# Recurrence and mixture of experts: where the second expert's first rows are gathered

## The chip, the cores and the metric

One core of one Trainium2 chip. The metric is the device time of one execution in microseconds; runs are compared by their median.

## The reference

The inputs are six arrays for 4 batches, 8 heads, 768 steps and a head width of 40, and the weights of 8 experts. First a recurrence over the steps with a 40 x 40 state for each batch and head, then a top-1 mixture of experts on its output:

```python
for t in range(S):
    y[:, :, t] = einsum('bhd,bhde->bhe', rt, state)
    Sa = einsum('bhde,bhe->bhd', state, at)
    state = state * wt - outer(Sa, bt) + outer(vt, kt)
x = y.transpose(0, 2, 1, 3).reshape(3072, 320)      # tokens
e_idx = argmax(x @ w_gate); gate_w = softmax(x @ w_gate) at e_idx
out[tokens of e] = gate_w * sigmoid(x @ w_output_gate)[e] * (relu(x @ w1[e]) @ w2[e])   # 320 -> 1024 -> 320
```

All of it is float32.

## The kernel before

The recurrence is worked through in 12 chunks of 64 steps, each in two parts (batches of two) called q = 0 and 1. A chunk's preparation, the solve for its inner dependence and the output of the chunk before run interleaved (class Att). Each part's output tile `x` (128 tokens of 320) is written to a scratch array `xd` in DRAM, and at once its router logits are computed (Moe.route, lines 643 to 662).

After chunks 3, 7, 10 and 11 the tokens seen since the last time are assigned (Moe.pick, from line 664): VectorE finds each token's expert and its place in that expert's list, and GpSimd (POOL) scatters, with one indirect DMA per 128 tokens (L730), a record of each token into a table `tab` in DRAM with 480 slots for each expert. These are 8, 8, 6 and 2 scatters. All write the same table, and each waits until the one before has landed.

An expert's 480 slots are 4 tiles of 120 (TS). Because the first two tiles of experts 0 and 1 are filled by tokens of chunks 0 to 7 only, they can be worked on early: Moe.slots reads the table a first time after chunk 7 (L878, on POOL's queue) and converts it on VectorE (L880 and L882) into the index `ti`. Moe.tokens then gathers the rows of `xd` for some tiles into `xg` by indirect DMAs on POOL (L818, one for each tile of 120 rows), transposes them on TensorE (L826, three k blocks, one transpose for each tile and block), and splits them into a high part on ScalarE (`xh`, L828) and a low part on VectorE (`xl`, L829). Moe.expert multiplies by w1 in 8 feature blocks f of eight matmuls each (L850, in high and low parts), applies the relu into a high part on ScalarE (`hh`, L854) and a low part on VectorE (`hl`, L855), then for each tile multiplies by w2 in 24 matmuls (L865 to L867), scales the rows on VectorE (L869), and scatters them to the output on POOL (L870).

Moe.early runs along with the last chunks of the recurrence: it loads and splits expert 0's weights, gathers and transposes expert 0's first two tiles in a small pool `tp0`, in which the tag `xg` has one buffer, and works feature blocks 0 to 5 of expert 0. Moe.experts runs after the recurrence: it opens its own pools (among them `tp` with two buffers of each tag), finishes blocks 6 and 7 of expert 0 and its output, and goes on with expert 1's first two tiles, the second halves of experts 0 and 1, and experts 2 to 7 with four tiles each. While one unit computes, the transposes of the next unit and the weight splits (L778 to L784) of the next expert are taken in turn with it (unit). The second halves need the whole table: Moe.slots reads it a second time, on SP's queue, after the last scatter has landed.

Each engine works its own queue in order. The order in these queues is made by a planner that runs through the program with its own clock and takes what is ready, in program order where several are; `issue_after` adds a fixed order in a few places. A tile's buffer is given out again when the last reader of its old content is done.

Of the kernel before, what the change touches and what calls it, by code (L numbers as in the profile page):

```python
# [9 lines left out]
F32 = mybir.dt.float32  # L10
# [571 lines left out]
E, CAP, DM, FF, NTOK = 8, 480, 320, 1024, 3072  # L582
TS = CAP // 4
# [3 lines left out]
class Moe:  # L587
# [216 lines left out]
            for _ in range(lag):  # L804
                yield

    def tokens(s, tabs, e, t0, nt, pool, psx):

        nc = s.nc
        m = 2 if pool is s.tp0 else 4  # L810
        rows = 256 * (s.HALF + 1) if t0 + nt <= s.HT else NTOK
        xh = pool.tile([128, 3, TS * m], F32R, name="xh", tag="xh")[:, :, 0:TS * nt]
        xl = pool.tile([128, 3, TS * m], F32R, name="xl", tag="xl")[:, :, 0:TS * nt]
        xg = pool.tile([TS, m, DM], F32, name="xg", tag="xg")
        tb, ti = (x[:, :, 4 * e + t0:4 * e + t0 + nt] for x in tabs)
        yield tb, ti, xh, xl
        for t in range(nt):
            nc.gpsimd.indirect_dma_start(out=xg[:, t], out_offset=None, in_=s.xd[0:rows],  # L818
                                         in_offset=bass.IndirectOffsetOnAxis(ap=ti[:, 0, t:t + 1], axis=0),
                                         bounds_check=rows - 1, oob_is_err=True)  # L820
        yield
        for k in range(3):
            n = 128 if k < 2 else 64
            pt = psx(TS * nt)
            for t in range(nt):
                nc.tensor.transpose(out=pt[0:n, TS * t:TS * t + TS], in_=xg[:, t, 128 * k:128 * k + n],  # L826
                                    identity=s.ident[0:TS, 0:TS])
            nc.scalar.copy(out=xh[0:n, k], in_=pt[0:n])  # L828
            nc.vector.tensor_tensor(out=xl[0:n, k], in0=pt[0:n], in1=xh[0:n, k].bitcast(F32), op=ALU.subtract)  # L829
            if k == 2:  # L830
                nc.scalar.copy(out=xh[64:128, k], in_=pt[0:64])
                nc.scalar.copy(out=xl[64:128, k], in_=xl[0:64, k].bitcast(F32))
            yield

    def expert(s, nt, W, T, pool, ps1, ps2):

# [48 lines left out]
    def early(s, ctx, psx, mark):  # L885

        pool = lambda n, b: ctx.enter_context(s.tc.tile_pool(name=n, bufs=b, side="right"))
        s.wpa, s.tp0 = pool("wpa", 1), pool("tp0", 1)
        with s.tc.tile_pool(name="sp0", bufs=2, side="right") as sp:
            w = s.weights(0, s.wpa, sp, 12, mark)  # L890
            s.W0 = next(w)
            yield from w
        while not s.half:
            yield
        for _ in range(30):
            yield
        with s.tc.issue_after(mark['ds']):
            s.tabs = s.slots(s.tp0, s.nc.gpsimd)
        t = s.tokens(s.tabs, 0, 0, 2, s.tp0, psx)
        T = next(t)  # L900
        next(t)
        for _ in range(40):
            yield
        with s.tc.issue_after(mark['y']):
            next(t)
        yield from t
        s.hp0 = ExitStack()
        hp = s.hp0.enter_context(s.tc.tile_pool(name="hp0", bufs=E0, side="right"))
        s.hp = hp, TS * 2
        s.wait = {}  # L910
        s.E0 = s.expert(2, s.W0, T, lambda: s.hp, lambda: s.ps1(), lambda: s.ps2())
        s.ps1 = lambda: psx(CAP)
        for _ in range(4):
            next(s.E0)
            yield
        while 'over' not in mark:
            yield
        at = dict(a=mark['a'], b=s.at['g', 11, 0], c=mark['c'], d=s.at['t', 11, 1], e=s.at['g', 11, 1], f=s.at['p'])
        s.pins = {(4 + i // 8, i % 8): at[m] for i in range(8 * (E0 - 4)) for m in 'adee'[i // 4]}
        for _ in range(4, E0):  # L920
            next(s.E0)
            yield
        s.pins = {}

    def experts(s, ctx, verdict):
        tc = s.tc
        pool = lambda n, b, **k: ctx.enter_context(tc.tile_pool(name=n, bufs=b, **k))
        tp, wpb, sp, hp = pool("tp", 2), pool("wpb", 1), pool("sp", 4), pool("hp", 9)
        pp = pool("mps", 2, space=PSUM)
        psx = lambda n: pp.tile([128, CAP], F32, name="px", tag="px")[:, 0:n]  # L930
        ps1 = lambda: pp.tile([128, CAP], F32, name="ph", tag="ph", bufs=3)
        ps2 = lambda: pp.tile([TS, DM], F32, name="po", tag="po", bufs=3)
        s.hp, s.ps1, s.ps2 = (hp, CAP), ps1, ps2
        W, T = {0: s.W0}, {}

        def tok(tabs, *u):
            t = s.tokens(tabs, *u, tp, psx)
            T[u[:2]] = next(t)
            next(t)
            return t  # L940

        def wts(e, **k):
            w = s.weights(e, s.wpa if e % 2 == 0 else wpb, sp, **k)
            W[e] = next(w)
            return w

        def unit(e, t0, nt, prep):

            for _ in s.expert(nt, W[e], T[e, t0], lambda: s.hp, ps1, ps2) if (e, t0) != (0, 0) else s.E0:
                next(prep, None)  # L950
            for _ in prep:
                pass

        t = tok(s.tabs, 1, 0, 2)
        w = wts(1, st=s.st1)
        tabs = s.slots(tp)
        t2 = tok(tabs, 0, 2, 2)
        unit(0, 0, 2, chain(t, w))
        s.wait = None
        s.hp0.close()  # L960
        t3 = tok(tabs, 1, 2, 2)
        unit(1, 0, 2, t2)
        verdict(psx(1)[0:1])
        t = tok(tabs, 2, 0, 4)
        unit(0, 2, 2, t3)
        unit(1, 2, 2, chain(wts(2), t))
        for e in range(2, E):
            n = e + 1 < E
            t = tok(tabs, e + 1, 0, 4) if n else iter(())
            with ExitStack() as order:  # L970
                if not n:
                    order.enter_context(tc.manual_schedule(engines={mybir.EngineType.PE}))
                w = wts(e + 1) if n else t
                unit(e, 0, 4, chain(islice(w, 3), t, iter("  "), w) if n else t)
# [177 lines left out]
```

## Time and profile before

| | us |
|---|---|
| median of 3 runs (684.51 to 687.52) | 686.28 |
| the profiled execution's own time | 687.68 |
| its span, first to last instruction | 685.9 |
| TensorE busy | 633.7 |
| VectorE busy | 465.5 |
| ScalarE busy | 339.3 |
| GpSimd (POOL) busy | 228.0 |

Times in the rows are microseconds from the start of the span. TensorE's matmuls are pipelined, so one in the queue may start before the one before it has ended. The recurrence ends near 439 us; what follows are the experts. The clock granted to TensorE is 0.969 of the full one on average.

### The profile page before, as it was taken

The numbers are of one execution on the slowest core, as the hardware profiler recorded it, in microseconds if no ns is written. First come the engines' busy times: TensorE is split into PE (matmuls) and PEld (weight loads), VectorE is DVE, ScalarE is ACT, GpSimd is POOL, SyncE is SP. The second block draws the span as 40 slices with busy tenths as digits, with TensorE's granted clock in tenths as the row PEclk, the third lists the DMA queues.
The fourth block names the chain that finished last, engine by engine and source line by source line (L and its number), as shares of the span: only waits on it lengthen the run. The fifth ranks groups of instructions, "written<-read, shape, count | busy, mean of one in ns | idle before, by whom it ended". The sixth has DMA issues, their size and how long they took to land. (4 is left out here: it accounts for less than half of the span.)

```text
span 685.9 us, 21154 instructions
## 1 busy us (share of the span) xinstructions
PE 633.7 (92%) x8871; PEld 566.5 (83%) x8871; DVE 465.5 (68%) x911; ACT 339.3 (49%) x783; POOL 228.0 (33%) x337
## 2 busy tenths in 40 slices
PE   7686988898999999989999789889999999999996
PEld 6475877777988788888889779789999998999986
DVE  8868689959986997799399554463675445654231
ACT  2577752774378357637743354243563335343120
POOL 9655321341244356315214100425333133202112
PEclk9668999999999999999999999999999999999999
DMA  6995762276346626633225563163575444431001
GB/s 141 174 191 123 180 158 70 80 165 166 98 133 165 143 74 170 175 86 101 80 80 147 170 161 88 33 197 88 172 217 145 144 133 126 138 106 45 19 11 32
DMA packets 56305, 84.45 MB, mean 123 GB/s; under 512 B 26848, under 2 KB 43515, under 8 KB 54763
## 3 DMA queue, kind: packets, MB, share of 16 engines
q1 hardware_dynamic: 52331, 74.05, 41.3%
q0 software_dynamic: 3872, 8.97, 4.6%
q8 instruction: 72, 1.18, 0.7%
q14 instruction: 30, 0.25, 0.1%
HBM read 67.59 MB, written 8.96 MB: 112 GB/s over the span
## 5 line engine op out<-in xcount | busy, mean ns | idle before, releaser
L855 DVE SCALAR_TENSOR_TENSOR hl<-ph,hh 128x480 fp32r<-128x480 f32 (+1 forms) x74 | 41.2, 566 | 66.6 <-ACT hh L854 54.9
L854 ACT ACTIVATE hh<-ph 128x480 fp32r<-128x480 f32 (+1 forms) x74 | 36.5, 501 | 95.5 <-PE ph L850 83.6
L870 POOL DMA_INDIRECT out_dram<-y,ti x32 | 33.7, 1054 | 141.3 <-DVE y L869 87.0
L865 PE MATMUL po<-w2h,hh 128*120 128x320 f32 x256 | 78.7, 313 | 0.2 <-ACT hh L854 0.2
L866 PE MATMUL po<-w2l,hh 128*120 128x320 f32 x256 | 77.9, 310 | 0.0
L850 PE MATMUL ph<-xh,w1h 128*128 128x480 f32 (+1 forms) x222 | 76.6, 349 | 0.3 <-DVE base L700 0.3
L850 PE MATMUL ph<-xl,w1h 128*128 128x480 f32 (+1 forms) x222 | 76.1, 346 | 0.0
L867 PE MATMUL po<-w2h,hl 128*120 128x320 f32 x256 | 75.2, 309 | 0.0
L225 PE MATMUL pl<-Am,KBt 120*128 120x192 f32 (+1 forms) x288 | 62.7, 351 | 8.6 <-ACT LA L238 6.6
L240 POOL TENSOR_SCALAR_AFFINE_SELECT LA<-LA 64x192 f32<-64x192 f32 x144 | 54.1, 408 | 45.8 <-ACT LA L238 44.5
L383 ACT ACTIVATE As<-pa,hq 128x320 f32<-128x320 f32 x80 | 42.0, 528 | 48.0 <-PE pa L392 34.2
L236 ACT ACTIVATE N<-pl 32x192 f32<-32x192 f32 (+1 forms) x138 | 51.5, 373 | 27.9 <-PE pl L225 12.9
L730 POOL DMA_INDIRECT tab<-rec,si x24 | 29.6, 1235 | 91.7 <-DMA tab<-rec,si 40.0
L480 PE MATMUL pY<-KB,M 128*64 128x64 f32 (+1 forms) x768 | 54.4, 226 | 4.9 <-DVE M L468 3.5
L225 PEld LDWEIGHTS pl<-Am,KBt 120*128 120x128 f32 x288 | 47.0, 205 | 14.2 <-ACT LA L238 9.0
L392 PE MATMUL pa<-As,Tc 64*32 64x40 f32 x1792 | 51.0, 204 | 4.9 <-ACT As L383 4.8
L480 PEld LDWEIGHTS pY<-KB,M 128*64 128x64 f32 x768 | 47.6, 139 | 8.9 <-DVE M L468 4.0
L479 PE MATMUL pY<-Sd,R 128*64 128x64 f32 (+1 forms) x704 | 54.9, 228 | 0.0
L464 PE MATMUL pM<-R,VU 128*128 128x128 f32 x384 | 52.3, 287 | 0.9 <-ACT VU L456 0.8
L392 PEld LDWEIGHTS pa<-As,Tc 64*32 64x32 f32 x1792 | 40.2, 112 | 14.7 <-ACT As L383 5.2
L850 PE MATMUL ph<-xh,w1l 128*128 128x480 f32 (+1 forms) x148 | 51.0, 345 | 0.0
L464 PEld LDWEIGHTS pM<-R,VU 128*128 128x128 f32 x384 | 46.5, 195 | 2.7 <-ACT VU L456 1.2
(198 smaller groups left out, 1559.9 us busy)
## 6 DMA issues: line engine op xcount, KB each, us to landing
D<-in_din_dram SPq DMA_DIRECT2D x12, 1080.0 KB
st<-in_w_dram SPq DMA_DIRECT2D x16, 512.0 KB
st<-in_w_dram SPq DMA_DIRECT2D x16, 480.0 KB
XS<-in_vt_dram SPq DMA_DIRECT2D x24, 256.0 KB
XU<-in_vt_dram SPq DMA_DIRECT2D x24, 256.0 KB
VU<-in_vl_dram SPq DMA_DIRECT2D x24, 208.0 KB
w<-in_win_dram SPq DMA_DIRECT2D x12, 371.2 KB
st<-in_w_dram SPq DMA_DIRECT2D x16, 256.0 KB
```

The source lines that it names most:

```text
L225: nc.tensor.matmul(pl[:, i, 0:nj], KBt[:, 6 * side + g0 + i].rearrange("p n t -> p (n t)"), Am[:, g0 + i:g0 + i + 6 * nj - 5:6, 0:64], sta ...
L236: s.mark['n', c] = nc.scalar.activation(out=nn, in_=pn, func=AF.Copy, scale=-1.0).ins
L240: g.affine_select(out=la[:, :, i], in_=la[:, :, i], pattern=[[0, nj], [1, C]], base=0, channel_multiplier=-1, compare_op=ALU.is_gt, fill=0.0)
L383: s.mark['as'] = nc.scalar.activation(out=x, in_=pa, func=AF.Copy, scale=s.hq[:, h:h + 1]).ins
L392: nc.tensor.matmul(pa[o + w:o + w + 32, i], m(p)[o:o + 64], x[o:o + 64, i, :], start=start, stop=True, tile_position=(o, o + w), skip_grou ...
L464: nc.tensor.matmul(pM[:, i], VU[:, h0 + i].rearrange("p n t -> p (n t)"), R[:, :, h0 + i], start=True, stop=True)
L479: nc.tensor.matmul(o, R[:, side, i, :], Sf[:, 40 * i:40 * i + w], start=True, stop=False)
L480: s.mark['y'] = nc.tensor.matmul(o, Ms[i // 4][:, i % 4, side, :], Kf[:, k:k + w], start=not c, stop=True).ins
L850: nc.tensor.matmul(ph, l, r, start=(i == 0), stop=(i == 7))
L865: nc.tensor.matmul(po, hh[f][:, ts_], w2h[:, f], start=(f == 0), stop=False)
L866: nc.tensor.matmul(po, hh[f][:, ts_], w2l[:, f], start=False, stop=False)
L867: nc.tensor.matmul(po, hl[f][:, ts_], w2h[:, f], start=False, stop=(f == 7))
```

## The change

The gather is taken out of Moe.tokens into a function of its own, Moe.rows. Moe.early calls it for expert 1's first two tiles as soon as expert 0's transposes are in the program. The call allocates `xg` in `tp0`, whose one buffer is the one that expert 0's rows were in. Moe.experts hands the tile to Moe.tokens, which then gathers nothing for this unit. The tiles of all other units are gathered as before.

```diff
-    def tokens(s, tabs, e, t0, nt, pool, psx):
+    def tokens(s, tabs, e, t0, nt, pool, psx, gp=None):
         ...
-        xg = pool.tile([TS, m, DM], F32, name="xg", tag="xg")
         tb, ti = (x[:, :, 4 * e + t0:4 * e + t0 + nt] for x in tabs)
         yield tb, ti, xh, xl
-        for t in range(nt):
-            nc.gpsimd.indirect_dma_start(out=xg[:, t], out_offset=None, in_=s.xd[0:rows],
-                                         in_offset=bass.IndirectOffsetOnAxis(ap=ti[:, 0, t:t + 1], axis=0),
-                                         bounds_check=rows - 1, oob_is_err=True)
+        xg = gp or s.rows(tabs, e, t0, nt, pool)
         yield
...
+    def rows(s, tabs, e, t0, nt, pool):
+        nc = s.nc
+        m = 2 if pool is s.tp0 else 4
+        rows = 256 * (s.HALF + 1) if t0 + nt <= s.HT else NTOK
+        xg = pool.tile([TS, m, DM], F32, name="xg", tag="xg")
+        ti = tabs[1][:, :, 4 * e + t0:4 * e + t0 + nt]
+        for t in range(nt):
+            nc.gpsimd.indirect_dma_start(out=xg[:, t], out_offset=None, in_=s.xd[0:rows],
+                                         in_offset=bass.IndirectOffsetOnAxis(ap=ti[:, 0, t:t + 1], axis=0),
+                                         bounds_check=rows - 1, oob_is_err=True)
+        return xg
...
     def early(s, ctx, psx, mark):
         ...
         yield from t
+        s.xg1 = s.rows(s.tabs, 1, 0, 2, s.tp0)
         s.hp0 = ExitStack()
...
     def experts(s, ctx, verdict):
         ...
-        def tok(tabs, *u):
-            t = s.tokens(tabs, *u, tp, psx)
+        def tok(tabs, *u, **k):
+            t = s.tokens(tabs, *u, tp, psx, **k)
...
-        t = tok(s.tabs, 1, 0, 2)
+        t = tok(s.tabs, 1, 0, 2, gp=s.xg1)
```

## Rows read from the trace of the kernel before

**Rows 1.** TensorE's waits, 385 to 470 us, then 456 us to the end: total, times, longest

```profile
PE pa L392 <- ACT As L383: 4.1, 2, 2.7
PE px L826 <- DMA xg<-xd,ti: 2.7, 2, 1.5
...
PE po L865 <- ACT hh L854: 0.2, 1, 0.2
```

**Rows 2.** Timeline of TensorE, 445 to 455 us: start, us, instructions, idle time before

```profile
445.34 0.27 PE L850 MATMUL ph<-xl,w1h 128*128 128x240 f32 x1
446.81 0.29 PE L826 MATMUL px<-ident,xg 120*128 120x120 f32 x1 [1.20 <-DMA xg<-xd,ti]
448.62 0.32 PE L826 MATMUL px<-ident,xg 120*128 120x120 f32 x1 [1.51 <-DMA xg<-xd,ti]
448.70 0.40 PE L850 MATMUL ph<-xh,w1h 128*128 128x240 f32 x1
...
454.39 0.31 PE L867 MATMUL po<-w2h,hl 128*120 128x320 f32 x1
```

**Rows 3.** Windows: busy by engine, then TensorE's granted clock, DMA share, GB/s

```profile
442.00:445.00 3.00, 1.81 (x16) 1.48 (x16) 2.46 (x20) 0.78 (x4) 2.19 (x3) 1.00 0.01 1
448.00:453.00 5.00, 4.38 (x22) 4.39 (x23) 3.04 (x4) 3.97 (x6) 0.00 (x0) 0.66 0.92 320
453.00:456.00 3.00, 3.00 (x23) 2.97 (x22) 2.94 (x5) 2.41 (x5) 1.00 (x1) 1.00 0.11 39
```

**Rows 4.** Timeline of POOL, 380 to 463 us

```profile
390.61 0.62 POOL L878 DMA_DIRECT2D tr<-tab  x1 [7.25 <-issue]
...
427.39 1.03 POOL L730 DMA_INDIRECT tab<-rec,si  x1 [31.25 <-DVE rec L727]
...
442.20 0.97 POOL L730 DMA_INDIRECT tab<-rec,si  x1 [1.41 <-ACT LG L655]
...
444.91 1.11 POOL L818 DMA_INDIRECT xg<-xd,ti  x1 [0.31 <-issue]
446.33 1.03 POOL L730 DMA_INDIRECT tab<-rec,si  x1 [0.30 <-issue]
453.10 1.00 POOL L730 DMA_INDIRECT tab<-rec,si  x1 [5.75 <-DMA tab<-rec,si]
459.45 1.09 POOL L870 DMA_INDIRECT out_dram<-y,ti  x1 [5.35 <-DVE y L869]
...
462.28 1.10 POOL L818 DMA_INDIRECT xg<-xd,ti  x1 [0.31 <-issue]
```

**Rows 5.** Timeline of TensorE: other transposes of gathered rows, and what follows

```profile
419.12 0.37 PE L826 MATMUL px<-ident,xg 120*64 120x120 f32 x2
...
466.36 0.37 PE L826 MATMUL px<-ident,xg 120*128 120x120 f32 x2
466.49 0.38 PE L866 MATMUL po<-w2l,hh 128*120 128x320 f32 x1
```

**Rows 6.** Timeline of SP's queue: the second read of the table

```profile
455.25 0.34 SPq L878 DMA_DIRECT2D tr<-tab  x1
```

**Rows 7.** Timeline of VectorE, 392 to 460 us

```profile
392.70 0.28 DVE L880 COPY tb<-tr 120x128 f32<-120x128 f32 x1
...
445.55 0.16 DVE L713 SCALAR_TENSOR_TENSOR si<-mem 128x2 int32<-128x2 f32 x1
...
452.64 0.40 DVE L855 SCALAR_TENSOR_TENSOR hl<-ph,hh 128x240 fp32r<-128x240 f32 x1
...
458.88 0.55 DVE L869 TENSOR_SCALAR y<-po,tb 120x320 f32<-120x320 f32 x1 [0.32 <-PE po L867]
459.35 0.27 DVE L880 COPY tb<-tr 120x128 f32<-120x128 f32 x1
459.65 0.20 DVE L882 CAST ti<-tb 120x64 int32<-120x64 f32 x1
```

**Rows 8.** An idle stretch of TensorE in the recurrence, and the window behind it

```profile
390.05 0.76 PE L392 MATMUL pa<-As,Tc 64*32 64x40 f32 x32 [2.66 <-ACT As L383]
...
390.00:395.00 5.00, 4.95 (x105) 4.66 (x107) 3.79 (x7) 2.29 (x4) 1.80 (x3) 0.66 0.54 144
```

More of the change, by code (lines that the diff above doesn't have):

```diff
@@ L805, in weights @@
                 yield
-    def tokens(s, tabs, e, t0, nt, pool, psx):
+    def tokens(s, tabs, e, t0, nt, pool, psx, gp=None):
         nc = s.nc
         m = 2 if pool is s.tp0 else 4
-        rows = 256 * (s.HALF + 1) if t0 + nt <= s.HT else NTOK
         xh = pool.tile([128, 3, TS * m], F32R, name="xh", tag="xh")[:, :, 0:TS * nt]
         xl = pool.tile([128, 3, TS * m], F32R, name="xl", tag="xl")[:, :, 0:TS * nt]
-        xg = pool.tile([TS, m, DM], F32, name="xg", tag="xg")
         tb, ti = (x[:, :, 4 * e + t0:4 * e + t0 + nt] for x in tabs)
         yield tb, ti, xh, xl
-        for t in range(nt):
-            nc.gpsimd.indirect_dma_start(out=xg[:, t], out_offset=None, in_=s.xd[0:rows],
-                                         in_offset=bass.IndirectOffsetOnAxis(ap=ti[:, 0, t:t + 1], axis=0),
-                                         bounds_check=rows - 1, oob_is_err=True)
+        xg = gp or s.rows(tabs, e, t0, nt, pool)
         yield
```

## The prediction

> **What bounds the kernel now.** I read the page's first table first: TensorE is the fullest engine by far. An average says nothing about one place, so next came TensorE's waits. From 456 us to the end it waits 0.2 us in all [rows 1]: in that stretch its queue alone sets the end, and a microsecond won ahead of it is a microsecond off the kernel, as long as nothing else becomes late. In the stretch ahead (385 to 470 us) the second largest entry, 2.7 us, is two waits of the transposes of the second expert's first rows for the DMA that brings these rows [rows 1]. The timeline of TensorE shows the place: feature block 6 of the first expert issues its last matmul at 445.34, the two transposes stand at 446.81 and 448.62, and block 7, which needs nothing of them, stands behind them in the queue until 448.70 [rows 2]. The windows show what follows: the granted clock is 0.66 on average from 448 to 453 us, so for part of it at the lower of the two levels (1.2 GHz), and full again from 453 [rows 3]. POOL's timeline shows why the rows are late: the second gather is issued at 444.91, right behind a chain of scatters into the slot table that ends with the one at 442.20, while the same queue has nothing to do for 31.25 us before 427.39 [rows 4].
>
> **The change part by part.**
>
> *The two gathers move.* They keep their size and count (2 DMAs of 120 rows). They no longer fill a tile of the later pool, but the first expert's tile, so each now waits until the first expert's six transposes have read it. Those end at 419.12 + 0.37 = 419.5 [rows 5]. POOL is idle then, so two gathers of 1.11 us with 0.31 between [rows 4] would run from about 419.5 to 422.1 and land by 424.7 (the second one's landing now takes 2.6 us: issued until 446.02, used at 448.62 [rows 2, 4]). Queued behind this wait on POOL are the six scatters of chunks 8 to 10, the first of which can't start before 427.39 because it waits for its records [rows 4]: 5.3 us of cover. If that cover were gone the price would be 2.8 us on the scatters, of which about 1.3 is slack: the last of the six starts at 442.20, and one takes 2.15 us from start to landing (453.10 to the read of the table at 455.25 [rows 4, 6]), so it is down at 444.35, and the next scatter needs slots that exist only at 445.55 + 0.16 = 445.71 [rows 7]. I take 0. The gathers' traffic moves to a stretch with fewer loads; I take 0 there too.
>
> *The wait goes.* With the rows there, the two transposes follow block 6 at once, 0.11 us after its last matmul's start. A pair takes 0.13 us at the full clock (466.36 to 466.49 [rows 5]), so block 7 starts at 445.45 + 0.13 = 445.58 and not at 448.70: **3.12 us**, the two waits and the pipeline's emptying around them. The step of 0.11 is an estimate from the pair; with a whole matmul of 0.27 [rows 2] it would be 2.96.
>
> *The low clock goes.* TensorE is busy without a break after 448.70, and from 448 to 453 the clock lacks 0.34 x 5 = **1.70 us** [rows 3]. That it does not fall in the changed kernel is a choice: it is 1.00 from 442 to 445 [rows 3], where TensorE is busy for only 1.81 of 3 us, and what it did before it fell is 2.7 us of waiting within 3.1. If it fell all the same, 1.70 would be lost again.
>
> So TensorE could be 3.12 + 1.70 = 4.82 us earlier at 453 us. Two things can be late in its place.
>
> *VectorE and ScalarE behind the transposes.* Their work for the second expert starts with the split of the transposed rows and so comes forward with the transposes, by 448.62 - 445.5 = 3.1, not by 4.82. The low part of block 7 is written at 452.64 + 0.40 = 453.04 [rows 7] and needed by the last matmul of the first output group at 454.39 [rows 2]; shifted, it is there at 449.94 and wanted at 449.57: **0.4 us** late. Bounds: 0 (the planner may order VectorE otherwise) to 1.72 (nothing had slack); I take 0.4, since it is worked out from the two rows.
>
> *The rows of the first expert's second half.* This is the next gather, and it hangs on the slot table: scatters at 446.33 and 453.10, read of the table at 455.25, its conversion on VectorE at 459.35 and 459.65, the second gather at 462.28 [rows 4, 6, 7]. That gather ends at 463.38, lands 2.6 later at 465.98, and the transposes stand at 466.36 [rows 5]: 0.38 us of slack today. How far does the chain come forward? (a) The conversion stands behind two output scalings on VectorE (the last is at 458.88 [rows 7]), which wait for TensorE. The table read itself should be down 2.1 us after its issue, as the other one was (390.61 to 392.70 [rows 4, 7]), so at 457.35: 2.0 us are won once the scalings are earlier. (b) The gathers then don't stand behind an output scatter, which ends at 459.45 + 1.09 = 460.54 [rows 4], 0.7 after the index at 459.85 [rows 7]: 0.7. (c) The scatter at 446.33 landed only just before 453.10, while the weight loads kept the DMA engines 0.92 full from 448 to 453 [rows 3]. Without two gathers of 154 KB each in that stretch, 307 KB at its 320 GB/s, it lands some 1.0 us earlier. Bounds of (c): 0.45 (only its issue comes earlier, to just behind the slots) and 4.5 (it lands 2.15 us behind an unhindered issue). The sum is 3.7.
>
> The rule for (c) that stands against me is in the Trainium skill, DMA: Bandwidth & Descriptors, section on queues, rings and completion order: a DMA engine takes turns between its queues packet by packet, so a small scatter would share turns with the loads and need not wait for a backlog to drain. By that, taking bytes out of the backlog brings the scatter little, and the sum would end at 3.5. The row (landing at the very moment at which the DMA share falls, 0.92 before 453 and 0.11 after) speaks more for the backlog.
>
> **The sum.** TensorE alone would be 4.82 - 0.4 = 4.4 us earlier; the chain of the next rows allows 3.7 + 0.38 = 4.1. The smaller gain counts: **4.1 us**. The profiled execution took 687.68 us, of which 685.9 are the span; 687.68 - 4.1 = 683.6. It stands 1.4 above the median of the three runs (686.28), so on the median the forecast is **682.2 us**, 0.6% less.
>
> **The rivals.**
>
> *The next gather takes the wait over.* If neither (a) nor (b) nor (c) holds, the chain of the slot table stays where it is, and TensorE gains only the 0.38 of slack; with (a) and half of (c) it gains 2.9. For it: the slack of 0.38 is small and the three terms are inferred. Against it: the conversion on VectorE starts right behind the scaling, which waited for TensorE. Middle of it: 1.6 us, 684.7.
>
> *The change does not do what it says.* The order of POOL's queue is planned, and if the gathers are put behind the scatters of chunks 8 to 10, they run where they run today: 0, 686.3. For it: the scatters belong to older work. Against it: their records come 8 us after the transposes.
>
> *Slower: one long hole in place of two short ones.* If the chain of the table does not come forward at all and gathers put between the scatters make it late (2.8 - 1.3 = 1.5), TensorE is 4.4 early at the transposes of the second half and waits 4.4 - 0.38 + 1.5 = 5.5 us in one piece. A single idle stretch of 2.66 us ahead of 390.05 was followed by a clock of 0.66 over 390 to 395, which is 0.34 x 5 = 1.7 us lost [rows 8]. Net: 1.5 - 0.38 + 1.7 = 2.8 us slower, 689.1. It decides from the point where the hole is as long as those 2.66 us. It needs the planner to interleave the queue badly, which the 31 us gap on POOL makes unlikely.
>
> **How the numbers follow.** Chances: forecast 0.52, the next gather takes over 0.28, no effect 0.08, slower 0.12. The forecast's own range is 3.0 to 5.2 us of gain (4.8 with nothing late, and 0.4 if transposes fill holes between 442 and 445 us; 3.0 with (c) at 0.45 and the clock partly low), 681.1 to 683.3. The range for 8 in 10 reaches over the takeover and no effect: 680.8 to 686.9. About 0.5% is what a measurement of this kernel can tell from no change, 3.4 us, or 682.85: most of the forecast's range lies below it and a part above, which, with half a chance in the forecast and the medians' own spread, gives faster 0.50. Same gets 0.40 (the takeover, no effect, the weak end of the forecast and the mild part of the slower case), slower 0.10.
>
> **What would show it.** In the changed trace the two gathers stand on POOL at 419 to 423 us, ahead of the scatter that waits for its records; the transposes' wait for their rows is gone from TensorE's waits; the granted clock is 1.00 from 445 to 455; the conversion of the table moves by about 3 us on VectorE. Wrong: a new wait of TensorE for gathered rows between 455 and 470 us of over 1.5 us (the takeover), a clock of 0.5 behind it (the slower case), gathers behind 427 us (no effect), or a tail after 470 us that is no longer free of waits.

## The result, and the profile after

In 14 runs of each, the changed kernel took 680.87 us in the median (678.15 to 689.2) and the kernel before 687.34 (683.41 to 693.79). The ratio is 0.9902, 95% interval 0.9878 to 0.9925: 1.0% faster, 5.2 to 8.4 us. A gain of 4.1 us was forecast. The sign and the mechanism were right, the size was too small. Here and below, a few executions in a slower state are left out of the ratios. The profiled execution took 678.98 us.

Every engine's queue has the instructions of before in the order of before; only POOL's differs, by the two gathers, which now stand ahead of the six scatters. Their place on POOL, with the chain behind them (columns as in [rows 4]; L838 is the gather, L878 the output scatter):

```profile
416.28 1.09 POOL L838 DMA_INDIRECT xg<-xd,ti  x1 [21.70 <-PE px L821]
417.67 1.09 POOL L838 DMA_INDIRECT xg<-xd,ti  x1 [0.30 <-issue]
423.89 1.03 POOL L730 DMA_INDIRECT tab<-rec,si  x1 [5.12 <-DVE rec L727]
...
442.14 0.97 POOL L730 DMA_INDIRECT tab<-rec,si  x1 [2.43 <-DVE si L713]
446.81 1.47 POOL L730 DMA_INDIRECT tab<-rec,si  x1 [3.70 <-DMA tab<-rec,si]
452.39 1.04 POOL L878 DMA_INDIRECT out_dram<-y,ti  x1 [4.11 <-DVE ti L890]
...
455.18 1.11 POOL L838 DMA_INDIRECT xg<-xd,ti  x1 [0.31 <-issue]
```

They wait for the first expert's transposes, and their issue is over 5.1 us before the scatters can start. TensorE around block 6 (against [rows 2] and [rows 5]):

```profile
440.66 0.35 PE L858 MATMUL ph<-xh,w1h 128*128 128x240 f32 x1 [0.34 <-DVE mem L704]
...
441.64 0.37 PE L821 MATMUL px<-ident,xg 120*128 120x120 f32 x2
441.77 0.36 PE L858 MATMUL ph<-xh,w1h 128*128 128x240 f32 x1
...
446.54 0.31 PE L875 MATMUL po<-w2h,hl 128*120 128x320 f32 x1
...
450.18 0.27 PE L858 MATMUL ph<-xh,w1h 128*128 128x240 f32 x1
...
457.86 0.37 PE L821 MATMUL px<-ident,xg 120*128 120x120 f32 x2
```

Block 7 follows block 6 after 1.11 us, pair of transposes included. From block 6 to the second expert's first matmul (450.18) there are 9.52 us; in the kernel before it was 444.49 to 458.69, 14.20:

```profile
444.49 0.35 PE L850 MATMUL ph<-xh,w1h 128*128 128x240 f32 x1 [0.34 <-DVE base L700]
...
458.69 0.27 PE L850 MATMUL ph<-xh,w1h 128*128 128x240 f32 x1
```

The windows (columns as in [rows 3]) show the clock at 1.00 throughout:

```profile
442.00:445.00 3.00, 3.00 (x25) 3.00 (x24) 2.23 (x4) 3.00 (x6) 0.97 (x1) 1.00 0.57 179
445.00:448.00 3.00, 3.00 (x23) 2.97 (x22) 2.94 (x4) 3.00 (x5) 1.19 (x1) 1.00 0.97 329
448.00:453.00 5.00, 5.00 (x41) 4.84 (x39) 4.33 (x9) 1.32 (x5) 0.89 (x2) 1.00 0.51 147
```

VectorE converts the table at 451.88, with no idle time ahead of it ([rows 7] had 459.35):

```profile
445.76 0.40 DVE L863 SCALAR_TENSOR_TENSOR hl<-ph,hh 128x240 fp32r<-128x240 f32 x1
...
451.88 0.26 DVE L888 COPY tb<-tr 120x128 f32<-120x128 f32 x1
```

From the second expert's first matmul to the last one (679.02 before, 670.27 now) the two profiles take nearly the same, 220.33 us before and 220.09 after. So the two profiles differ by 4.68 us in the stretch of the change and by 0.24 behind it. The rest of the 8.7 us between their spans arose ahead of 440 us, most of it (3.5) before the gathers' new place, where both run the same instructions: chance. But the timed runs say more than 4.7, so the question was where the other 1 to 2 us are.

### The profile page after: what moved, and what is told of

It reads as the page before. It is cut to its first block, busy times and chain, and to the rows that moved or that the text cites. A ratio compares the mean times of both kernels' runs of the same rounds, so it can differ in the third digit from the quotient of the medians.

```text
span 677.2 us, 21154 instructions
## 1 busy us (share of the span) xinstructions
PE 630.9 (93%) x8871; PEld 564.3 (83%) x8871; DVE 464.9 (69%) x911; ACT 340.2 (50%) x783; POOL 233.8 (35%) x337
## 5 line engine op out<-in xcount | busy, mean ns | idle before, releaser
L878 POOL DMA_INDIRECT out_dram<-y,ti x32 | 34.3, 1073 | 141.5 <-DVE y L877 80.8
L838 POOL DMA_INDIRECT xg<-xd,ti x32 | 35.8, 1118 | 44.6 <-PE px L821 32.7
```

## The experiments

All stretches below run from block 6's first matmul to the second expert's first. "Gather issued" is the start of the second gather's issue; this time and that of its transpose are counted from block 6. They are read from each kernel's timelines:

| profile | gather issued | its transpose | stretch |
|---|---|---|---|
| kernel before, on record | 0.42 | 4.13 | 14.20 |
| b3_before_p3 | 0.69 | 5.28 | 15.21 |
| b4_before_p4 | 0.81 | 5.67 | 16.71 |
| b2_before_p2 | 0.82 | 5.71 | 16.61 |
| b5_before_p5 | 0.99 | 5.79 | 17.08 |
| b2_before_p1 | -1.69 | 1.40 | 9.89 |
| changed, 4 profiles | -22.99 | 1.1 (pair) | 9.52 each |

What stands ahead of block 6 counts, too. From the first expert's first transposes to block 6 the changed kernel takes 27.07 us in all four profiles, and the kernel before 27.07 to 27.47 in the five with a hole: the gathers cost nothing in their new place.

**The kernel before, five more profiles.**

> The kernel before once more, for a second profile of its stretch from block 6 of the first expert to the second expert's first matmul, which took 14.20 us in the profile on record and 9.52 in three profiles of kernels with early gathers. Theory A (the landing of the second gather, and so the hole, differs from one execution to the next, and the profile on record had a short one): 15 to 17 us here. Theory B (the stretch always costs 4.7 us and the rest of the measured gain is elsewhere): 14.0 to 14.4 us.

> The kernel before, for a third profile, with the same expectations: theory A 15 to 17 us for the stretch, theory B 14.0 to 14.4 us.

> The kernel before, for a fourth profile. The stretch from block 6 to the second expert's first matmul took 14.20, 9.89 and 16.61 us in the three so far. Theory A (a race: the hole is there when the two gathers are issued later than the weight loads' start less some 2.5 us, and absent when the scatter chain ran 2 us ahead): the stretch is near 10 with gathers issued over 3 us before block 6, or 14 to 17 with gathers issued less than 1.1 us before it. Theory B (the hole has nothing to do with the time of issue): any other pairing.

> The kernel before beside them, a fifth profile. Theory A (race with the loads): the time from the second gather's issue to its transpose lies on the line of the other three, 3.7 at 0.42 us after the start of block 6 to 4.9 at 0.82, or no wait at all with an issue over 1.5 us before block 6. Theory B (no tie to the time of issue): off this line by over 0.6 us.

> The kernel before beside it, a sixth profile. Theory A: with the second gather issued 0.4 to 0.9 us after block 6 begins, 3.7 to 5.0 us from there to its transpose and a stretch of 14 to 17 us; with an issue over 1.5 us before block 6, no hole and a stretch near 9.9. Theory B: any other pairing.

The profile on record was the mildest of the five with a hole, as theory A had it, and one has next to none (9.89 us in b2_before_p1), which neither theory of that run foresaw; theory A of the later three takes it in, and they agree with it (b5_before_p5 at its edge). The longest hole, b5_before_p5: TensorE's wait, then the windows.

```profile
PE px L826 <- DMA xg<-xd,ti: 4.2, 2, 2.6
```

```profile
443.00:446.00 3.00, 1.22 (x9) 1.08 (x9) 1.74 (x15) 0.58 (x2) 2.39 (x3) 0.80 0.27 63
446.00:449.00 3.00, 0.44 (x2) 0.16 (x3) 0.00 (x0) 0.00 (x0) 0.55 (x1) 0.50 0.99 331
449.00:454.00 5.00, 5.00 (x22) 5.00 (x23) 3.57 (x5) 4.53 (x8) 1.46 (x1) 0.50 0.54 204
454.00:457.00 3.00, 3.00 (x20) 2.97 (x18) 2.97 (x4) 1.95 (x4) 0.04 (x1) 0.82 0.08 21
```

Its wait is 4.2 and not 2.7 us, and the clock is at the lower level for all of the 5 us behind it. The weight loads on SP are issued at 1.40 to 1.45 after block 6 in these five, because they wait for the slots that VectorE writes then. An issue takes 1.1 us, so the gather is still being issued when the loads start; the one on record has 0.1 us left, those issued 0.3 to 0.6 us later have more, and their rows take 4.6 to 4.9 us from issue to transpose and not 3.7. In b3_before_p3 and b5_before_p5 the trace has the landings: the first gather, whose issue ends 0.8 to 1.0 us ahead of the loads, lands 3.1 us after the start of its issue, the second one 4.5 and 4.8 us. POOL in b2_before_p1, the one without a hole:

```profile
437.88 0.97 POOL L730 DMA_INDIRECT tab<-rec,si  x1 [1.41 <-DMA tab<-rec,si]
439.16 1.13 POOL L818 DMA_INDIRECT xg<-xd,ti  x1 [0.30 <-issue]
440.60 1.11 POOL L818 DMA_INDIRECT xg<-xd,ti  x1 [0.31 <-issue]
443.78 1.03 POOL L730 DMA_INDIRECT tab<-rec,si  x1 [2.07 <-DVE si L713]
```

From the second on, its scatters follow each other every 2.4 us; in the others one of these steps takes 2.9 to 3.6. And TensorE is later: the recurrence's last but one output takes 0.8 us longer on its way from M to x (2.45 us, 1.7 in the others). So here the gathers come 2.1 us or more earlier against block 6, and are through before the loads begin. Such an execution is still behind the changed kernel: from the first expert's first transposes to the second expert's first matmul it takes 38.31 us (28.42 of them ahead of block 6), the changed kernel 36.59.

**The changed kernel again, three times.**

> The changed kernel itself, for more executions beside the others and a second profile of the stretch. Between the two profiles on record, the stretch from block 6 of the first expert to the second expert's first matmul is 4.7 us shorter, as the forecast's two terms on TensorE said (4.82), but the 14 runs say 6.7 us (5.2 to 8.4). Theory A (the hole in front of the transposes is longer in most executions than in the one profiled): 5.5 to 7 us faster again, with no wait for gathered rows and a clock of 1.00 here. Theory B (the measured effect was lucky, the true one is the 4.7 of the profiles): 4.2 to 5.2 us faster.

> The changed kernel beside them, as the yardstick on the same chip, and a third profile: 9.5 us from block 6 to the second expert's first matmul as in the other two (theory A), 4 to 7 us below the kernel before in most chips and less where the kernel before has executions without the hole.

> The changed kernel once more, on whatever chip comes, beside the kernel before. In the two calls where the kernel before ran at 687.7 and 686.7 us the changed one gained 0.9% and 0.8%; in the two where it ran at 683.9 us, three of its profiles or those of kernels with its order had the gathers issued 2.1 us earlier and no hole, and the changed kernel was not among the runs. Theory A (the gain is the hole, and there is less of it where the kernel before often escapes it): near 681 to 682 us in any case, 0.8 to 1.0% faster if the kernel before is near 687, and 0.2 to 0.6% if it is near 684. Theory B (the chip's level moves both kernels alike): 0.8 to 1.0% faster wherever the kernel before lies.

Medians 681.51, 682.09 and 679.71, ratios 0.9912 (0.9884 to 0.9941), 0.9917 (0.9886 to 0.9948) and 0.9897 (0.9855 to 0.9938). The stretch is 9.52 us in every profile. Against the five profiles with a hole that is 4.7 to 7.6 us, 6.4 in the mean; by their ratios the timed runs gave 5.7 to 7.1. The first of these runs alone (4.1 to 8.0 us) allows both of its theories; the four measurements together, weighted by their intervals, say 6.4 us (5.4 to 7.4), which is theory A: the missing 1 to 2 us are longer holes. On the two chips where the kernel before was profiled beside it, profile and time agree (5.69 and 5.7 us in b3, 7.56 and 7.1 in b5). Whether the gain shrinks on chips where the kernel before often has no hole could not be seen, and so the theories of b5_after can't be told apart: on these three chips it ran at 686.7 to 687.7 us. All four profiles with the gathers early in the old place (b2_before_p1, b2_held6 and both of b4_late_loads) are from two other chips, where it ran at 683.9 us and the changed kernel was not run.

**Only the place undone.** The kernel is the changed one, but with the gathers behind a given scatter:

```diff
-        s.xg1 = s.rows(s.tabs, 1, 0, 2, s.tp0)      # in early
...
+        with s.tc.issue_after(s.at['s', 8, 5]):     # in experts; the sixth scatter (3: the fourth, 4: the fifth)
+            s.xg1 = s.rows(s.tabs, 1, 0, 2, s.tp0)
```

> The changed kernel (rows in the first expert's tile) with the two gathers held on POOL behind the sixth scatter of chunks 8 to 10, their place in the kernel before; every queue has the order of the kernel before. Theory A (only the time of issue matters): as slow as before, within 0.4%, with the transposes waiting 2.5 to 5 us for their rows and the clock at half rate behind it. Theory B (the tile matters, since the later pool's tile also waits for memory of the recurrence): 2 to 5 us faster than before.

Ratio 1.0002 (0.9963 to 1.0041): the time of the kernel before, so the tile alone is worth at most 2.5 us here and probably nothing. The profile itself fell on an execution without a hole (issue at -1.69, stretch 10.04, 0.3 us of waiting), as did b2_before_p1 on the same chip, where the kernel before ran at 683.89 us. Theory A is right on the time; the hole it expected was not in this one profile. How much the place is worth on this chip is not shown, since the changed kernel was not run there.

> The same with the gathers held behind the fourth scatter only, so that the fifth and sixth scatter stand behind them. Theory A: the rows land at about the end of block 6, so TensorE's wait and the low clock are gone or nearly gone; the scatters end later, but the last of the six has slack and the two gathers then no longer stand ahead of the scatters of chunk 11: 4 to 6.5 us faster than before, within 1.5 us of the changed kernel. Theory B (gathers between the scatters make the slot table late, as the slower rival of the forecast has it): a new wait of TensorE of over 2 us between 455 and 470 us, and 0 to 3 us faster than before only.

Ratio 1.0038 (0.9998 to 1.0079), against both theories. The rows were there in time and the stretch was 9.52, but the recurrence's last output took 3.69 us from M to x in place of 1.35, with gaps that wait for nothing the profile shows:

```profile
PE pY L480 <- issue: 0.7, 2, 0.4
PE pY L479 <- issue: 0.6, 2, 0.3
```

From the first expert's first transposes to block 6 this profile takes 30.44 us, 3.4 more than the changed kernel, so what the stretch gained was lost ahead of it. The gathers' rows were moving just then, which was the reason for the next two runs.

> The changed kernel with the two gathers held on POOL behind the fifth of the six scatters of chunks 8 to 10. Behind the sixth, in the old place, the time was that of the kernel before; behind the fourth the rows were there in time (no wait, clock 1.00), but TensorE lost 2.3 us to gaps marked as issue in the last output of the recurrence while the gathers' rows were moving. Behind the fifth the gathers run some 2.5 us later, mostly after that output. Theory A (two things cost: rows that are not there at the end of block 6, and rows that move while the recurrence's last output is issued): no hole before block 7 and under 1 us of issue gaps, within 1 us of the changed kernel. Theory B (any place among the scatters costs): 2 us or more slower than the changed kernel.

> The changed kernel with two more gathers of the same rows, into a tile that nothing reads, behind the fourth scatter. Theory A (moving 307 KB by POOL's queue while TensorE issues the many small matmuls of the last output keeps TensorE's instructions from coming): the last output, from the second masked product M to x on VectorE, takes 3 us and more in place of 1.35, and the kernel is 1.5 to 3 us slower than the changed one. Theory B (the gaps in that stretch were chance): under 0.7 us slower, with the stretch at 1.3 to 1.8 us.

b3_extra4 adds two gathers that nobody reads behind the fourth scatter:

```diff
+        with s.tc.issue_after(s.at['s', 8, 3]):
+            s.rows(s.tabs, 1, 0, 2, s.tp0, "xq")
         t = tok(s.tabs, 1, 0, 2, gp=s.xg1)
```

Its last output took 1.35 us from M to x, so theory A of b3_extra4 is not borne out. But this does not clear the gathers: on the chips of b2 and b4 the last output takes 1.6 to 1.7 us in every other profile, whatever the kernel, on the chip of b3 1.35 in all four, so the chip may have a part in it. What stopped TensorE in b2_held4 stays open. Both kernels are slower than the changed one beside them in the median, by 1.4 us (b3_held5, between its two theories) and 1.0 us (b3_extra4), though the intervals overlap (0.9951, 0.9922 to 0.9981, and 0.9938, 0.9907 to 0.9970, against 0.9917, 0.9886 to 0.9948). In the profiles the reason is another one. VectorE and POOL in b3_held5:

```profile
447.44 0.99 DVE L877 TENSOR_SCALAR y<-po,tb 120x320 f32<-120x320 f32 x2
451.98 0.27 DVE L888 COPY tb<-tr 120x128 f32<-120x128 f32 x1 [3.54 <-DMA tr<-tab]
452.28 0.19 DVE L890 CAST ti<-tb 120x64 int32<-120x64 f32 x1
452.39 1.03 DVE L863 SCALAR_TENSOR_TENSOR hl<-ph,hh 128x240 fp32r<-128x240 f32 x3
```

```profile
436.49 1.03 POOL L730 DMA_INDIRECT tab<-rec,si  x1 [0.30 <-issue]
440.91 1.15 POOL L730 DMA_INDIRECT tab<-rec,si  x1 [3.39 <-DMA tab<-rec,si]
447.53 0.98 POOL L730 DMA_INDIRECT tab<-rec,si  x1 [5.47 <-DMA tab<-rec,si]
```

The sixth scatter stands behind the gathers, so the scatters of chunk 11 run at 440.91 and 447.53 (4.1 and 10.8 us after block 6, against 1.5 and 6.2 in the changed kernel), and the table is late. Its conversion is in VectorE's queue ahead of the second expert's `hl`, waits 3.54 us, and TensorE waits for `hl` (in b3_extra4 the same two waits are 3.52 and 2.19 us). That wait, and the clock behind it (columns as before):

```profile
PE ph L858 <- DVE hl L863: 2.2, 1, 2.2
```

```profile
445.00:450.00 5.00, 4.76 (x38) 4.57 (x38) 3.44 (x7) 1.27 (x6) 2.02 (x2) 1.00 0.09 32
450.00:455.00 5.00, 2.83 (x16) 2.55 (x16) 1.64 (x6) 0.65 (x3) 1.25 (x2) 0.85 0.82 218
455.00:460.00 5.00, 5.00 (x36) 5.00 (x35) 1.10 (x4) 1.25 (x4) 4.09 (x4) 0.81 0.48 140
```

This is the forecast's slower rival, in a milder form and through VectorE: from the second expert's first matmul to the last these two profiles take 224.03 and 225.28 us, against 220.32 in b3_after_ref. The medians differ by less, so these two executions were worse than most.

**Early gathers, with the old ones left in place.**

```diff
+        s.rows(s.tabs, 1, 0, 2, tp)
         t = tok(s.tabs, 1, 0, 2, gp=s.xg1)
```

> The changed kernel with the two gathers issued a second time at their old place, into a tile that nothing reads. The early rows are the ones used, so TensorE's wait is gone, but POOL's queue and the DMA traffic beside the weight loads are as before. Theory A (all of the gain is TensorE's wait and its clock): as fast as the changed kernel, within 0.5 us. Theory B (part of the gain is that the slot table's scatters and the next gather come earlier without the two gathers): 1 to 2.5 us slower than the changed kernel, with TensorE waiting for gathered rows between 455 and 470 us.

681.98 us, ratio 0.9924 (0.9896 to 0.9953), half a microsecond above the changed kernel beside it. The stretch is again 9.52, so the wait is what counts. But the table's conversion comes 1.4 us later against block 6 (12.73, 11.35 in b1_after_again), and the next gather's transposes wait longer than there. First this run, then b1_after_again:

```profile
PE px L821 <- DMA xg<-xd,ti: 0.9, 1, 0.9
```

```profile
PE px L821 <- DMA xg<-xd,ti: 0.5, 1, 0.5
```

So theory A for the time, and 0.4 us of theory B in the profile (0.8 in all from the second expert's first matmul to the last, 221.53 and 220.73): this is about what the traffic and POOL's queue are worth, by one execution of each.

**Late gathers, but other work ahead of the transposes that wait.**

```diff
-            for _ in s.expert(...) if (e, t0) != (0, 0) else s.E0:
-                next(prep, None)
+            for i, _ in enumerate(s.expert(...) if (e, t0) != (0, 0) else s.E0):
+                if (e, t0) != (0, 0) or i >= 2:
+                    next(prep, None)
```

> The kernel before with the gathers where they were, but with block 7 and the first output tile of the first expert ahead of the second expert's transposes in TensorE's queue, some 4.4 us of work. Theory A (the cost is only that work which needs none of the rows stands behind the wait): the wait of 2.7 us and the low clock go without an earlier gather, 4 to 6.5 us faster than before. Theory B (the lateness of the rows itself is on the path, since VectorE and ScalarE split them and the weights behind them): under 2 us faster, with new waits of TensorE for xh or xl near 455 us.

684.12 us, ratio 0.9954 (0.9924 to 0.9984): 3.2 us faster than before, half of the change's gain. The stretch is 9.95, but a new wait stands behind it, and on VectorE its cause:

```profile
PE ph L850 <- DVE xl L829: 2.3, 1, 2.3
```

```profile
453.41 0.27 DVE L880 COPY tb<-tr 120x128 f32<-120x128 f32 x1 [2.58 <-DMA tr<-tab]
453.60 0.71 DVE L829 TENSOR_TENSOR xl<-px,xh 128x240 fp32r<-128x240 f32 x2
```

Again the conversion of the late table blocks VectorE's queue, here for the second expert's `xl`. Each theory has half: TensorE's order removes the hole, and the late rows come back as a wait for `xl`.

**A hole with TensorE kept busy.**

```diff
+            if f == 6 and s.wait is not None:
+                fl = ps2()
+                with s.tc.issue_after(mm):                       # block 6's last matmul
+                    for _ in range(20):
+                        nc.tensor.matmul(fl, hh[0][:, 0:TS], w2h[:, 0], start=True, stop=True)
```

> The kernel before with 20 matmuls that nobody reads (some 2.9 us of work) between block 6 and the transposes that wait. The wait keeps its place and length, but TensorE is busy through it. Theory A (the clock falls because of the hole): the clock is 1.00 from 445 to 455 us and the time is 1.0 to 2.0 us below before. Theory B (the clock's fall is chance and not tied to the hole, or costs nothing): within 0.5 us of before.

687.75 us, ratio 0.9998 (0.9970 to 1.0025). In the profile the gather was issued at 0.77, its transpose still waited 1.4 us behind the filler, and the clock stayed at 1.00. The stretch is 14.08, where kernels before with an issue at 0.69 and 0.81 had 15.21 and 16.71. But a new wait of 0.8 us for the next gather's rows stands behind it, since the order of VectorE's queue changed too. So the stretch speaks for theory A and the time for theory B, whose interval reaches to 2.1 us faster. What the clock alone is worth is inconclusive.

**Weight loads held until the rows have landed.**

```diff
+        pr = s.dr.tile([TS, 8], F32, name="pr")
+        s.probe = nc.sync.dma_start(out=pr, in_=s.xg1[:, 1, 0:8]).ins    # xg1: the second expert's xg
...
+                    if st:
+                        order.enter_context(s.tc.issue_after(s.probe))
```

> The kernel before with one small store of the second gather's rows put ahead of the four weight loads in SP's queue, so that these loads (480, 320 and twice 512 KB) start only when the rows have landed; nothing else moves. In the kernel before the second gather took 3.7, 4.6 and 4.9 us from its issue to the transposes that wait for it when it was issued 0.42, 0.69 and 0.82 us after block 6 began, and the loads were issued 1.40 after it each time; the first gather took 3.2 to 3.3. Theory A (its rows stand behind the weight loads on the DMA engines, and the later it is issued the more of them): 3.2 to 3.5 us from issue to transposes whatever the time of issue, a stretch of 13.5 to 14.3 us, and 0.5 to 2 us faster than before. Theory B (the rows' landing does not depend on the loads): 3.7 to 4.9 us as before, a stretch of 14.2 to 16.6, no faster than before or slower by the later loads.

> The same kernel, a second profile, same expectations: theory A 3.2 to 3.5 us from the issue of the second gather to its transpose, theory B 3.7 to 4.9 us.

682.91 us, ratio 0.9984 (0.9960 to 1.0008), and 683.64 in the single execution of the second. In both profiles the gathers were issued early (-1.69), so there was no race to take away: inconclusive. The loads' part in the hole rests on the table and the landings above, not on an intervention, and it need not be the whole: in b1_second_gather the first of the late gathers landed only 4.6 us after the start of its issue, though that issue ended 1.0 us ahead of the loads. One profile showed something else: a wait of only 0.20 us, and yet a low clock behind it.

```profile
440.00:444.00 4.00, 2.59 (x22) 2.05 (x20) 2.37 (x14) 1.53 (x5) 2.86 (x3) 1.00 0.26 80
444.00:446.00 2.00, 1.75 (x12) 1.57 (x13) 1.55 (x14) 0.58 (x2) 0.46 (x1) 0.84 0.34 85
446.00:449.00 3.00, 3.00 (x15) 3.00 (x15) 2.12 (x4) 2.96 (x5) 0.96 (x2) 0.54 0.45 76
```

## Why the prediction was right in kind and wrong in size

- **The bound**: right. TensorE's queue alone sets the end from 456 us; whatever the stretch gained or lost arrived at the end (220.0 to 220.3 us from the second expert's first matmul to the last in every profile with no wait for rows, `xl` or `hl` in it, 220.7 to 225.3 in those with one).
- **The gathers' move**: right, at no cost (27.07 us ahead of block 6, not more than before), and at the place that was forecast (between the transposes and the scatter that waits for its records).
- **The wait**: the step that failed is that a single profile's hole was taken as the size. 3.12 us was right for that execution (block 7 at 4.21 us after block 6, now 1.11), but it was the shortest of five: block 7 stood at 5.41 in b3_before_p3 and at 5.92 in b5_before_p5, so this term is 3.1 to 4.8 us. One execution of six had next to none (0.15 us of waiting).
- **The low clock**: 1.70 was 1.58 in that execution (4.68 - 3.10), 1.39 in b3_before_p3 (5.69 - 4.30) and 2.75 with the longest hole (7.56 - 4.81). That it would stay at 1.00 was right in all four profiles of the changed kernel. The ground given, that short holes don't lower it, was weak: in b4_late_loads it fell after pauses without a long hole.
- **VectorE's 0.4 us**: not there. A row was misread: the matmul at 454.39 [rows 2] is that of block 6; the ones that need block 7's `hl` follow the transposes after it. In the changed kernel `hl` is written by 446.16 and wanted at 446.54.
- **The next rows' 0.3 us**: not there in this profile, so TensorE's 4.8 came through undiminished (4.68), but with nothing to spare. The chain came forward by 3.3 us at its second gather (17.79 us after block 6 before, 14.52 now), nearly the 3.7 that were forecast, though with other parts: (b) did not happen, the gathers still stand behind the output scatter at 452.39, and (c) was larger (the last scatter came 2.5 us earlier against block 6, not 1.0). What was wrong is the slack of 0.38: the two transposes at 466.36 [rows 5] need only the first of the two gathers. Those that need the second are the next pair, at 467.16. In the changed kernel these pairs stand at 457.86 and 458.66, and the second gather, issued at 455.18, lands 3.4 us later (the last number of its row), at 458.6, 2.3 us after the end of its issue:

```profile
467.16 0.37 PE L826 MATMUL px<-ident,xg 120*128 120x120 f32 x2
```

```profile
458.66 0.42 PE L821 MATMUL px<-ident,xg 120*128 120x120 f32 x2
```

```profile
xg<-xd,ti POOLq DMA_INDIRECT x1, 3.4
```

By the same 2.3 the slack before was about 1.5 us (463.38 + 2.3 against 467.16; an estimate, the profile before lacks this landing), and all of it is used up now. So it was in part luck that nothing was lost: in b1_after_again TensorE waits 0.5 us here, the rival of the takeover in a mild form.
- **The rule for (c) in the Trainium skill** (DMA: Bandwidth & Descriptors, section on queues, rings and completion order), that a small transfer shares turns with the loads and gains little from a smaller backlog. The trace of the changed kernel agrees with the first half: the scatter issued at 442.14 landed 3.9 us later, at 446.0, while the DMA engines stayed 0.97 full from 445 to 448. The row that was read against it was misread: the scatter of 446.33 [rows 4] stood behind two gathers in POOL's own queue. With them put back (b1_second_gather) it landed 5.8 us after its issue, and 3.9 in b1_after_again beside it; these 1.9 us are most of (c).
- **The slower rival** needs gathers between the scatters; put there, they made the table late as described, and cost 1.4 and 1.0 us in the medians against the changed kernel (b3_held5, b3_extra4; not clear of noise). Both are still faster than the kernel before.

In sum: the forecast's 4.1 and the 0.7 us of the two deductions that were not there make 4.8, of which the two profiles show 4.7; the 1 to 2 us that the timed runs show above that are holes longer than the one profiled.

What stays open: why in some executions the scatters run 2.1 us or more ahead (one step takes 2.4 and not 2.9 to 3.6 us, and the recurrence's last but one output takes 0.5 to 0.8 us longer), how often that is, whether the gain is smaller where it is often, and what stopped TensorE in b2_held4.

## What to carry to other kernels

When the stall to be removed ends with a DMA that is issued close to others, profile several executions before sizing it: here, among profiles of one kernel, the one with the issue 0.6 us later had a loss of 7.6 us in place of 4.7, and the one with the issue 2.1 us earlier had almost none. Before a landing is set against the instruction that needs it, make sure which of several alike instructions that is: here two of the transposes need the first gather only, and the slack read from them was 0.4 us and not 1.5. A load that an in-order queue must convert (here the table on VectorE) passes its lateness on to everything behind it (3.54 us in b3_held5); placing the conversion behind the work that it could block was not tried.

## What was not expected of the hardware

A gather of 120 rows of 1,280 bytes landed 3.1 us after the start of its issue, 2.0 after its end, when it was alone (the two early gathers of the changed kernel), and 4.5 and 4.8 us after the start when four weight loads of 1.8 MB in all were issued while it was itself being issued (b3_before_p3, b5_before_p5). And the clock's fall isn't tied to one long pause: in b4_late_loads TensorE, busy for 2.59 of 4 us and then 1.75 of 2 with no wait above 0.6 us, ran at half clock from about 445.4 to 448.8; in b4_late_loads2, with the same kernel and a wait of 0.19 us, the clock stayed at 1.00.
